# The first eight head pairs of a fused attention and MLP kernel: scores one pair ahead of values, attended rows turned one pair later, and a reordered opening

## The chip, the cores and the metric

One core of one Trainium2 chip runs the kernel. The metric is the device time of one execution in microseconds (us), as the median of several executions. A profile is one further execution of its own, taken with the hardware profiler; its times are measured from the first instruction of the span.

## The reference

`q`, `k`, `v` have 8 batches, 8 heads, 576 positions and a head size of 64. Each position attends to positions at most 32 away, to 8 global positions, and the 8 global positions attend to all. The attended rows of all heads, 4608 x 512, then go through an MLP whose inner function is h times cos(h).

```python
scores = scale * np.matmul(q, k.transpose(0, 1, 3, 2))
mask = np.abs(pos[:, None] - pos[None, :]) <= window
mask = mask | is_global[:, None] | is_global[None, :]
scores = np.where(mask, scores, -1000000000.0)
attn = exp(scores - max) / sum
x = (attn @ v), heads side by side      # 4608 x 512
h = x @ w_in                            # 512 -> 2048
out = (h * np.cos(h)) @ w_out           # 2048 -> 512
```

## The kernel before

**Tiling.** Two heads make a pair; there are 32 pairs, four of them to a batch. The steps of a pair have one letter each, and a string spells out the order in which they are issued; every engine takes its own instructions in that order.

- `k`, `q` (`local_k` L574, `local_q` L585): for the first eight pairs, 16 transposes on TensorE each (L571), for pairs 0 to 3 also 16 small matmuls that pick the rows of global positions (L308), and copies of the result out of PSUM. In `local_q` the copies are a small one on VectorE (L591) and then the large one on ScalarE (L592).
- `s` (`scores5` L597): 10 matmuls (L607) into four PSUM banks, two exponentials for the first two banks (L610) and two for the others (L614) on ScalarE, three products with the mask on VectorE (two of L611, then L615).
- `p` (`values5` L617): 20 matmuls (L622) into the one accumulator `pv`, a small sum and two reciprocals (L636 to L638), and the division that writes the attended rows `xn` (L642), all on VectorE.
- `x` (`turn_x5` L646): five transposes of `xn` (L654), copies into `xT` and a sum for the global rows on VectorE (L655, L658, L660). After a batch's last pair GpSimd writes eight columns of `xT` (L663).
- `f` fills: 128x184 matmuls on ones (L470), which write into `pv` and are overwritten. `warm` (L311) is 128x512 matmuls on ones.
- `C` turns the loaded `v` rows into fp16 (`cast_vn`, L391 on GpSimd, for the first load L393 and L394 on VectorE and ScalarE). `H` and `g` bring the global rows into `kw` and `qb`; `H1` holds two transposes (L530) and two copies (L532). `Z` builds the mask of the later pairs.
- `L`, `W`, `O`, `c`, `K` are transfers issued by GpSimd: k and q of a half batch, a quarter of `w_in`, the whole of `w_out` (L851, 2048 KB as it lands), and v, k and q cast to fp16 in device memory (L264, L268). `B` is issued by SyncE: transposing loads of such a cast half (L280, L281) and its values.
- `1`/`m` is one step of the first MLP matmul (four 128x512 matmuls, L738), with its cosine and product (L744, L745) at once or at `t`; `2` is a quarter of a 128-row step of the second (four matmuls, L755), which needs `w_out`.

**Order.** `FRONT` (L57) has pairs 0 to 7 and four MLP steps. `MID` (L49) is MLP alone while `w_out` arrives; after it `FOURTH`, `FIFTH` and `SIXTH` each run two pairs of later batches with MLP steps between, and from there `ORDER` repeats. Only two row tiles of the MLP, 32 steps of `1`, can be done until the iteration of `SIXTH`. In `FRONT` before, pair n+1's scores stand behind pair n's values, and k and q of a pair two or so ahead directly behind a pair's scores:

```
... s4 g6 g7 k6 q6 f4 x3 c4 K4 p4 s5 C3 k7 q7 f4 x4 p5 s6 W2 W3 f4 x5 p6 s7 B4 K5 O m m x6 p7 ...
```

PSUM has three banks for scores and turned rows together (tag `s`), one more for scores (`o`), two for k and q (`h`) and two for `pv`.

Of the kernel before, what the change touches and what calls it, by code (L numbers as in the profile page):

```python
# [12 lines left out]
AF = mybir.ActivationFunctionType  # L13
# [8 lines left out]
QB = 56  # L22
# [182 lines left out]
def kernel(  # L205
# [152 lines left out]
    def vn_of(s):  # L358
        return view(vn32[s // 2][:, 4 * (s % 2)], (4 * D, NK5), (1, 4 * D))
# [381 lines left out]
    def mlp_act():  # L741
        ph, g = ph_of.pop(0)
        cos = work.tile([P, TT], FP16, tag="cos", bufs=3)
        nc.scalar.activation(cos, ph, AF.Sin, bias=pio2)  # L744
        nc.vector.tensor_tensor(g, cos, ph, ALU.mult)  # L745
# [107 lines left out]
    STEPS = {"s": scores, "p": values, "x": turn_x}  # L853
    with tc.manual_schedule():

        nc.vector.memset(ones16, 1.0)
        nc.vector.memset(pio2, pi / 2.0)
        nc.vector.memset(kn[0][0:KPAD, 0:2], 0.0)
        nc.vector.memset(qn[0][64:QP, 0:2], 0.0)
# [4 lines left out]
        load_qk(0, (0, 2))  # L864
        for t in (kn[0][0:KPAD, 2:4], qn[0][64:QP, 2:4], kn[1][0:KPAD], qn[1][64:QP]):
            nc.scalar.memzero(t.rearrange("p a b c -> p (a b c)"))
        nc.scalar.activation(x_sq[:, 0:1], pio2, AF.Exp)
        nc.gpsimd.iota(tok_i, pattern=[[1, RW]], base=0, channel_multiplier=RW)
        nc.gpsimd.memset(ident16, 1.0)
        nc.gpsimd.affine_select(ident16, ident16, [[-1, P]], ALU.is_equal, 0.0, base=0, channel_multiplier=1)  # L870
        warm(WARM)
        index_rows(0)
        build_band()
        load_qk(0, (2, 4))
        for s in range(HY):
            nc.vector.memset(vn_of(s)[0:32, 0], 0.0)
        load_vn(0)
        index_rows(1)
        gather(v, vg32, 0)
        load_qk(1)  # L880
        gather(k, kg32, 0)
        gather(q, qg32, 0)
        nc.gpsimd.iota(kid_i, pattern=[[QB, NB]], base=-(G + 32), channel_multiplier=1)
        nc.gpsimd.iota(d_i, pattern=[[-1, C]], base=0, channel_multiplier=1)
        load_vn_rows(0)
        for s in range(1, HY):
            load_vn(s)
            load_vn_rows(s)
        build_ones()
        build_mask5()  # L890
# [8 lines left out]
        local_k(0)  # L899
        local_q(0)  # L900
# [36 lines left out]
        def bring(s):  # L937
# [2 lines left out]
            load_values(2 * s)  # L940
            load_values(2 * s + 1)

        LOCAL = {"k": local_k, "q": local_q}
        OTHER = LOCAL | {"g": globals_kq, "L": load_qk, "W": load_w_in, "c": lambda s: cast_half(s, "v"), "v": load_values, "n": x_squares,
                 "C": cast_vn, "V": lambda _: hold(9), "H": early_globals, "Z": steady_buffers, "f": fill, "r": load_vn, "A": later_rows, "D": later_globals, "O": load_w_out, "K": lambda s: cast_half(s, "kq" if s == 4 else "vkq"), "B": bring, "m": lambda _: one(False), "t": lambda _: mlp_act()}
        ready[0] = 1
        for step in FRONT.split():
            if step in "+-":
# [89 lines left out]
```

## Time and profile before

| | us |
|---|---|
| median of 3 runs | 368.34 (366.97 to 368.53) |
| the profiled execution | 366.35 |
| its span, first to last instruction | 364.4 |
| TensorE busy | 336.9 (92%) |
| VectorE busy | 250.2 (69%) |
| ScalarE busy | 235.6 (65%) |
| GpSimd busy | 105.7 (29%) |

The profile's page divides the span into 40 slices of 9.1 us. A row of the timeline gives start, length, engine, line, operation, output and inputs, count, and in brackets how long the engine stood idle before it and what ended that.

### The profile page before, as it was taken

What the parts mean: (1) busy time and instruction counts of PE and PEld (TensorE: products, weight loads), DVE (VectorE), ACT (ScalarE), POOL (GpSimd) and SP (SyncE); (2) the same over time, 40 slices, a digit from 0 to 9 for tenths busy, and PEclk for the clock granted to TensorE, in tenths of its full rate; (3) what the DMA queues carried; (4) which work ended last, traced back from release to release, by engine and by line L of the source; (5) the groups of instructions that cost most, each with busy time, mean ns of one, the idle gap of its engine ahead of it and who ended that gap; (6) DMA issues with size and microseconds to landing.
All of it is one profiled execution on the core that took longest, in us unless ns stands there. A gap on an engine that the chain in (4) does not pass through costs nothing.

```text
span 364.4 us, 8183 instructions
## 1 busy us (share of the span) xinstructions
PE 336.9 (92%) x3081; PEld 173.2 (48%) x3081; DVE 250.2 (69%) x607; ACT 235.6 (65%) x397; POOL 105.7 (29%) x217
## 2 busy tenths in 40 slices
PE   6597979979877999999999999999999999999993
PEld 3486735435443444444544444454544444444441
DVE  7465778966767868887878788797968444455410
ACT  5556656886732887768686777877778756644400
POOL 8634494452507322440515070502001100000000
PEclk9556789999989999999999999999999999999998
DMA  6999599999999999999999999999910000100121
GB/s 92 177 160 193 92 131 162 183 215 143 144 197 144 194 166 149 168 129 181 130 198 129 196 123 174 136 192 146 105 50 30 31 29 29 59 29 30 40 78 65
DMA packets 175655, 45.73 MB, mean 126 GB/s; under 512 B 163897, under 2 KB 170617, under 8 KB 175417
## 3 DMA queue, kind: packets, MB, share of 16 engines
q1 hardware_dynamic: 111753, 27.57, 53.6%
q0 software_dynamic: 63856, 17.57, 49.3%
q8 instruction: 26, 0.43, 0.5%
q14 instruction: 20, 0.16, 0.2%
HBM read 45.07 MB, written 20.05 MB: 179 GB/s over the span
## 4 chain that ended last, share of the span: by engine, by line
PE 68%; DMA 8%; ACT 6%; issue 6%; DVE 5%; POOL 5%; POOLq 0%; ACTq 0%
PE po L755 31%; PE ph L738 25%; DMA w_out<-in_moe_w_out_dram 8%; PE st L675 3%; PE tx L720 2%; ACT e L678 2%; POOL q L268 2%; PE pv L695 2%; ACT e L683 1%; POOL k L268 1%; PE bank L571 1%; POOL v L264 1%; PE pn L787 1%; PE st L607 1%; DVE xn L706 1%
## 5 line engine op out<-in xcount | busy, mean ns | idle before, releaser
L738 PE MATMUL ph<-xT,w_in 128*128 128x512 f16 x576 | 142.3, 382 | 1.8 <-issue 0.8
L755 PE MATMUL po<-w_out,g 128*128 128x512 f16 x576 | 140.7, 382 | 1.8 <-DMA w_out<-in_moe_w_out_dram 1.8
L744 ACT ACTIVATE cos<-ph,pio 128x512 f16<-128x512 f32 x144 | 96.8, 686 | 61.5 <-PE ph L738 59.1
L745 DVE TENSOR_TENSOR g<-cos,ph 128x512 f16<-128x512 f16 x144 | 95.5, 684 | 47.2 <-ACT cos L744 46.5
L755 PEld LDWEIGHTS <-g 128*128 128x128 f16 x576 | 55.3, 98 | 67.6 <-DMA w_out<-in_moe_w_out_dram 2.3
L738 PEld LDWEIGHTS <-w_in 128*128 128x128 f16 x576 | 54.5, 98 | 66.2 <-issue 7.3
L928 POOL COPY gate<-xn 1x1 f16<-1x1 f16 x12 | 2.2, 181 | 134.7 <-DVE xn L706 134.7
L678 ACT ACTIVATE e<-st 128x512 f16<-128x512 f32 x48 | 26.1, 595 | 16.9 <-PE st L675 16.8
L679 DVE TENSOR_TENSOR pm<-e,mask 128x512 f16<-128x512 f16 x48 | 20.3, 425 | 20.7 <-ACT e L678 19.2
L268 POOL DMA_DIRECT2D q<-in_q_dram x12 | 27.6, 2296 | 0.0
L760 ACT COPY o<-po 128x512 f32<-128x512 f32 x18 | 10.5, 585 | 22.3 <-PE po L755 22.0
L706 DVE TENSOR_TENSOR xn<-pv,r_all 128x768 f16<-128x768 f32 x24 | 23.0, 958 | 1.1
L773 ACT ACTIVATE xn<-xn 128x1536 f16<-128x1536 f16 (+1 forms) x16 | 22.8, 1423 | 0.0
L268 POOL DMA_DIRECT2D k<-in_k_dram x12 | 21.2, 1765 | 0.2 <-issue 0.2
L762 DVE COPY o<-po 128x512 f32<-128x512 f32 x18 | 12.4, 689 | 10.5 <-PE po L755 9.9
L728 POOL COPY xT<-xg 128x4 f16 x48 | 15.8, 329 | 5.5 <-DVE xT L723 2.9
L583 DVE COPY kw<-kT 128x1320 f16<-128x1320 f16 x24 | 17.1, 713 | 0.0
L610 ACT ACTIVATE e<-st 128x488 f16<-128x488 f32 x16 | 8.4, 575 | 11.8 <-PE st L607 11.8
L675 PEld LDWEIGHTS <-kw 64*128 64x128 f16 x528 | 9.2, 95 | 13.9 <-issue 8.3
L744 ACT ACT_TABLE_LOAD x12 | 15.4, 1283 | 0.2
L675 PE MATMUL st<-qb,kw 64*128 64x64 f16 x528 | 12.1, 191 | 3.5 <-POOL xT L728 2.3
L720 PEld LDWEIGHTS <-xn 128*128 128x128 f16 x144 | 9.2, 99 | 11.0 <-DVE xn L706 9.9
(168 smaller groups left out, 367.3 us busy)
## 6 DMA issues: line engine op xcount, KB each, us to landing
out_dram<-o SPq DMA_DIRECT2D x36, 256.0 KB
vw<-v SPq DMA_DIRECT2D x35, 165.0 KB
v<-in_v_dram POOLq DMA_DIRECT2D x12, 288.0 KB
k<-in_k_dram POOLq DMA_DIRECT2D x12, 288.0 KB
q<-in_q_dram POOLq DMA_DIRECT2D x12, 288.0 KB
w_in<-in_moe_w_in_dram POOLq DMA_DIRECT2D x4, 512.0 KB
w_out<-in_moe_w_out_dram POOLq DMA_DIRECT2D x1, 2048.0 KB
vn<-in_v_dram SPq DMA_DIRECT2D x16, 120.0 KB
```

The costliest lines, as they stand in the source:

```text
L268: nc.gpsimd.dma_start(dst[s].rearrange("t (h d) -> t h d", h=4), dview(src, base, (D, S), (S * D, 4), (1, D)))
L583: nc.vector.tensor_copy(to, view(kT[pr // 2 % 2][:, pr % 2], (QB, NB), (1, W)))
L675: nc.tensor.matmul(st[j // 8 * 2 + h][:, j % 8 * C : j % 8 * C + C], kp[hp, j], qp[hp, j], start=True, stop=True)
L678: nc.scalar.activation(e[:, 0:512], st[h], AF.Exp, scale=scale)
L679: nc.vector.tensor_tensor(view(pm[:, h], (1, 512)), e[:, 0:512], view(mask, (1, 512)), ALU.mult)
L706: nc.vector.tensor_tensor(view(xn, (384, 2), (D, 6), (1, D)), view(pv, (512, 2), (65, 6), (1, D)), view(rp, (6, 2), (1, 6), (0, D)), ALU.mult)
L720: nc.tensor.transpose(tx[:, n], xn[:, n], ident16)
L738: nc.tensor.matmul(ph, w_in16[:, j, f * P : (f + 1) * P], xT[:, j, t * TT : (t + 1) * TT], start=(j == 0), stop=(j == NC - 1))
L744: nc.scalar.activation(cos, ph, AF.Sin, bias=pio2)
L745: nc.vector.tensor_tensor(g, cos, ph, ALU.mult)
L755: nc.tensor.matmul(po, g16[:, f, s * P : (s + 1) * P], w_out16[:, f], start=(f == 0), stop=(f == NF - 1))
L773: nc.scalar.activation(view(xn, (BP * P, 2), (1, n)), view(xn, (BP * P, 2), (1, n)), AF.Square, accum_out=x_sq[:, s : s + 1])
```

## The change

The opening is put in another order: the first loads of k and q go out ahead of GpSimd's index patterns, memsets that only later steps need stand behind the first pair, `warm(4)` and `warm(6)` stand beside the first pair's k and q, and `w6` behind the second's; values of the second half batch are loaded ahead of the first's global rows, and the gather of q comes later. In `FRONT` the scores of pair n+1 stand in front of the values of pair n, the turn of attended rows comes behind those values and is that of pair n-1, and behind it come k and q of pair n+2. The fills between pairs 4 and 7 are gone. All of `w_in` is requested inside `FRONT`; the casts of half 4 are held (`U7`, a one-element copy on GpSimd) until the last mask product of pair 7. `w_out` is requested at the start of `MID`, which on GpSimd's queue is behind the column writes of batch 1 and the global rows of pairs 8 and 9, and the casts of half 5 come after it. `MID` has 18 steps of the first MLP matmul in place of 22; the four that are missing are taken up by `FOURTH` (two more) and `FIFTH` (two).

```diff
-MID = "+ 1 1 1 1 Z1 1 1 1 1 A0 n0 Z2 1 1 A1 kc qc 1 1 kd qd V K6 1 1 A2 n1 1 1 B5 1 1 n2 1 1 1 1 -"
+MID = "+ O 1 1 1 1 Z1 K5 1 1 1 1 A0 n0 Z2 1 1 A1 kc qc 1 1 kd qd V K6 1 1 A2 n1 1 1 B5 n2 1 1 -"
...
-FRONT = ("s0 k1 q1 C0 Z0 L2 W0 f8 s1 p0 k2 q2 f4 x0 p1 s2 C1 k3 q3 L3 W1 H0 f4 x1 p2 s3 k4 q4 H1 g4 g5 C2 k5 q5 x2 p3 "
-         "s4 g6 g7 k6 q6 f4 x3 c4 K4 p4 s5 C3 k7 q7 f4 x4 p5 s6 W2 W3 f4 x5 p6 s7 B4 K5 O m m x6 p7 t t + m m t t x7 -")
+FRONT = ("s0 k1 q1 w6 C0 L2 Q s1 p0 k2 q2 Z0 f8 s2 p1 x0 C1 W0 k3 q3 L3 H0 f4 s3 p2 x1 H1 g4 g5 k4 q4 C2 W1 f4 s4 p3 x2 "
+         "g6 g7 k5 q5 s5 p4 x3 k6 q6 C3 W2 s6 p5 x4 k7 q7 W3 s7 p6 x5 U7 c4 K4 B4 m m x6 p7 t t + m m t t x7 -")
...
+    def hold_pm(pr):
+        nc.gpsimd.tensor_copy(gate, pm_of[pr][0:1, 2 * CN - 1 : 2 * CN])
...
+        nc.vector.memset(qn[0][64:QP, 0:2], 0.0)
         nc.vector.memset(ones16, 1.0)
         nc.vector.memset(pio2, pi / 2.0)
         nc.vector.memset(kn[0][0:KPAD, 0:2], 0.0)
...
+        load_qk(0, (0, 2))
         nc.gpsimd.iota(p_i, pattern=[[0, 1]], base=0, channel_multiplier=1)
...
+        load_qk(0, (2, 4))
+        nc.scalar.activation(x_sq[:, 0:1], pio2, AF.Exp)
         warm(WARM)
         index_rows(0)
+        nc.vector.memset(vn_of(0)[0:64, 0], 0.0)
         build_band()
+        index_rows(1)
         load_vn(0)
         gather(v, vg32, 0)
         load_qk(1)
         gather(k, kg32, 0)
+        build_ones()
+        build_mask5()
+        local_k(0)
+        warm(4)
+        local_q(0)
+        warm(6)
+        for s in range(1, HY):
+            nc.vector.memset(vn_of(s)[0:32, 0], 0.0)
+        load_vn(1, 0, 3)
         load_vn_rows(0)
+        load_vn(1, 3)
+        load_vn_rows(1)
...
+        def late_gather(_):
+            gather(q, qg32, 0)
...
```

More of the change, by code (lines that the diff above doesn't have):

```diff
@@ L858 @@
         nc.vector.memset(kn[0][0:KPAD, 0:2], 0.0)
-        nc.vector.memset(qn[0][64:QP, 0:2], 0.0)
+        for t in (qn[0][64:QP, 2:4], kn[0][0:KPAD, 2:4], qn[1][64:QP], kn[1][0:KPAD]):
+            nc.scalar.memzero(t.rearrange("p a b c -> p (a b c)"))
+        load_qk(0, (0, 2))
         nc.gpsimd.iota(p_i, pattern=[[0, 1]], base=0, channel_multiplier=1)
@@ L863 @@
         nc.gpsimd.iota(kid5_i, pattern=[[KS, NK5]], base=-(G + 24), channel_multiplier=1)
[L864 to L868, printed above, removed]
         nc.gpsimd.memset(ident16, 1.0)
         nc.gpsimd.affine_select(ident16, ident16, [[-1, P]], ALU.is_equal, 0.0, base=0, channel_multiplier=1)
+        nc.gpsimd.iota(tok_i, pattern=[[1, RW]], base=0, channel_multiplier=RW)
+        load_qk(0, (2, 4))
+        nc.scalar.activation(x_sq[:, 0:1], pio2, AF.Exp)
         warm(WARM)
         index_rows(0)
+        nc.vector.memset(vn_of(0)[0:64, 0], 0.0)
         build_band()
-        load_qk(0, (2, 4))
-        for s in range(HY):
-            nc.vector.memset(vn_of(s)[0:32, 0], 0.0)
+        index_rows(1)
         load_vn(0)
-        index_rows(1)
         gather(v, vg32, 0)
@@ L881 @@
         gather(k, kg32, 0)
-        gather(q, qg32, 0)
-        nc.gpsimd.iota(kid_i, pattern=[[QB, NB]], base=-(G + 32), channel_multiplier=1)
-        nc.gpsimd.iota(d_i, pattern=[[-1, C]], base=0, channel_multiplier=1)
+        build_ones()
[7 more added lines that the diff above has]
+        load_vn(1, 0, 3)
         load_vn_rows(0)
-        for s in range(1, HY):
+        load_vn(1, 3)
+        load_vn_rows(1)
+        for s in range(2, HY):
             load_vn(s)
             load_vn_rows(s)
-        build_ones()
-        build_mask5()
         pv = ps.tile([P, 2, 512], FP32, tag="pv", bufs=1)
@@ L941, in bring @@
             load_values(2 * s + 1)
+        def late_gather(_):
+            gather(q, qg32, 0)
+            nc.gpsimd.iota(kid_i, pattern=[[QB, NB]], base=-(G + 32), channel_multiplier=1)
+            nc.gpsimd.iota(d_i, pattern=[[-1, C]], base=0, channel_multiplier=1)
         LOCAL = {"k": local_k, "q": local_q}
         OTHER = LOCAL | {"g": globals_kq, "L": load_qk, "W": load_w_in, "c": lambda s: cast_half(s, "v"), "v": load_values, "n": x_squares,
-                 "C": cast_vn, "V": lambda _: hold(9), "H": early_globals, "Z": steady_buffers, "f": fill, "r": load_vn, "A": later_rows, "D": later_globals, "O": load_w_out, "K": lambda s: cast_half(s, "kq" if s == 4 else "vkq"), "B": bring, "m": lambda _: one(False), "t": lambda _: mlp_act()}
+                 "C": cast_vn, "w": warm, "Q": late_gather, "U": hold_pm, "V": lambda _: hold(9), "H": early_globals, "Z": steady_buffers, "f": fill, "r": load_vn, "A": later_rows, "D": later_globals, "O": load_w_out, "K": lambda s: cast_half(s, "kq" if s == 4 else "vkq"), "B": bring, "m": lambda _: one(False), "t": lambda _: mlp_act()}
         ready[0] = 1
```

2 lines of the change are left out of this document (removed).

## The prediction

> **What bounds the kernel now.** I read the page, then stretches of the timeline, then the order in which each engine gets its instructions. The page and a table of stretches (busy time and count of each engine, granted clock, DMA share, GB/s) come first.
>
> ```profile
> span 364.4 us, 8183 instructions
> ...
> PE 68%; DMA 8%; ACT 6%; issue 6%; DVE 5%; POOL 5%; POOLq 0%; ACTq 0%
> ```
>
> ```profile
> core 0: us, PE busy (x) PEld busy (x) DVE busy (x) ACT busy (x) POOL busy (x), PEclk, DMA share, GB/s
> 24.00:27.00 3.00, 3.00 (x69) 2.52 (x69) 2.13 (x8) 1.55 (x4) 1.25 (x1) 0.50 1.21 197
> 58.00:79.00 21.00, 19.68 (x93) 8.62 (x90) 19.10 (x45) 17.86 (x29) 10.42 (x20) 1.00 1.54 182
> 97.60:113.40 15.80, 11.59 (x132) 5.81 (x133) 11.53 (x24) 5.97 (x12) 5.04 (x8) 0.89 1.57 172
> 113.40:133.00 19.60, 19.43 (x195) 9.53 (x196) 14.55 (x33) 13.91 (x26) 7.58 (x18) 1.00 1.65 165
> ```
>
> From 113.4 us TensorE is busy 19.43 of 19.60 us, and both kernels have the same TensorE order from the iteration of `SIXTH`, which starts there. So nothing after 113.4 us can change by much: the change is worth what it does to the moment at which that state is reached. Before it lie the eight pairs, the MLP steps of `MID`, and the stretch from 97.6, where TensorE is busy 11.59 of 15.80 us.
>
> The next rows mark the pairs: the first exponentials of pairs 1 and 7, two of seven such rows.
>
> ```profile
> 18.42 1.05 ACT L610 ACTIVATE e<-st 128x488 f16<-128x488 f32 x2 [0.21 <-PE st L607]
> ...
> 51.36 1.04 ACT L610 ACTIVATE e<-st 128x488 f16<-128x488 f32 x2 [3.25 <-PE st L607]
> ...
> 52.13 3.55 POOL L851 DMA_DIRECT2D w_out<-in_moe_w_out_dram  x1
> ...
> 80.59 1.90 PE L755 MATMUL po<-w_out,g 128*128 128x512 f16 x8 [1.84 <-DMA w_out<-in_moe_w_out_dram]
> ```
>
> Six pairs take 51.36 - 18.42 = 32.94 us, 5.49 each. `w_out` is requested at 52.13, and the second MLP matmul starts when it lands, 80.59, that is 29.2 us after pair 7's first exponential; TensorE waits only 1.84 us there, because `MID` has kept it busy. I call these two moments E7 and Y. My sum is: where E7 goes, how far behind it Y lies, and what the four postponed MLP steps cost.
>
> **The change part by part.**
>
> *The new loop of a pair.* The orders of the engines show what moves. ScalarE's large copy of q waits for VectorE's small one; the chain rows below show it, L591 ending at 40.89 and L592 starting at 40.93. Before, k and q stood right behind a pair's scores, so that L591 came directly after the mask products. In the changed kernel VectorE's order in each round is: three mask products of pair n+1, sum, reciprocals and division of pair n, three turned copies of pair n-1, and only then the small q copy of pair n+2; the scores of n+2 are next on TensorE and need that q. So each round closes a ring. Its links, from one pair of the run before:
>
> ```profile
> 39.12 0.78 DVE L611 TENSOR_TENSOR pm<-e,qT 128x488 f16<-128x488 f16 x2
> 40.26 0.56 DVE L615 TENSOR_TENSOR pm<-e,qT 128x768 f16<-128x768 f16 x1 [0.35 <-ACT e L614]
> 40.73 0.16 DVE L591 COPY qb<-bank 128x8 f16<-128x8 f16 x1
> 41.10 0.47 DVE L655 COPY xT<-tx 128x600 f16<-128x600 f16 x1 [0.20 <-PE tx L654]
> 41.49 0.15 DVE L658 COPY xT<-tx 128x8 f16<-128x8 f16 x1
> 41.55 0.18 DVE L660 TENSOR_REDUCE xg<-tx 128x8 f16<-128x32 f16 x1
> 42.14 0.15 DVE L636 TENSOR_REDUCE dg<-pv 8x2 f32<-8x8 f32 x1 [0.40 <-PE pv L622]
> 42.22 0.20 DVE L637 RECIPROCAL r_all<-pv 128x10 f32<-128x10 f32 x1
> 42.45 0.19 DVE L638 RECIPROCAL r_all<-dg 8x8 f32<-8x8 f32 x1
> 42.68 0.82 DVE L642 TENSOR_TENSOR xn<-pv,r_all 128x640 f16<-128x640 f32 x1
> ```
>
> ```profile
> 17.74 0.91 PE L607 MATMUL st<-qb,kw 64*128 64x136 f16 x10
> ...
> 38.41 1.04 ACT L610 ACTIVATE e<-st 128x488 f16<-128x488 f32 x2 [1.74 <-PE st L607]
> ...
> 40.93 0.66 ACT L592 COPY qb<-bank 128x600 f16<-128x600 f16 x1 [0.15 <-DVE qb L591]
> ```
>
> First exponential to the end of the mask products: 40.82 - 38.41 = 2.41. Sum to division: 42.14 to 43.50, 1.36. Turned copies: 41.10 to 41.73, 0.63. Small and large q copy: 40.73 to 41.59, 0.86. From the first scores matmul to the first exponential: 17.74 to 18.42, 0.68 at half clock. The sum is 5.94 us. Shown lengths of neighbours overlap by about 0.1, so I take 5.8 a round. Bounds: 5.5, if a full clock halves the 0.68, and 6.2, if nothing overlaps and each of the five handovers costs 0.05. The matmuls of values, turns, k and q lie beside VectorE's part of the ring and cost nothing; that cover holds while TensorE's work for a pair fits in a round, and at half clock with fills it filled 3.00 of 3.00 us (24 to 27), so the cover is thin. Six rounds: 34.8 us, against 32.94 before.
>
> *What the rounds have besides.* With `H1` two copies stand ahead of the small q copy on VectorE, and k and q of pair 4 need the two banks that these free.
>
> ```profile
> L532 DVE COPY kgT<-t x1: 225/225/225, 34.0 to 34.0; 128x128 f16<-128x128 f16 x1
> ```
>
> The two alone are 0.45 us; behind them now also come pair 4's transposes and ScalarE's copy of its k (0.66, as that of q above), and I take +1.4 (bounds 0.45 and 2). The cast `C3` comes behind GpSimd's eight column writes of batch 0, by my count just in pair 6's mask products:
>
> ```profile
> L391 POOL CAST vw<-vn x3: 1248/1259/2606, 24.0 to 46.7; 128x1280 f16<-128x1280 f32 x3
> ```
>
> ```profile
> 47.21 2.36 DVE L611 TENSOR_TENSOR pm<-e,qT 128x488 f16<-128x488 f16 x2
> ```
>
> The three casts took 1.25, 1.26 and 2.61 us; beside the slow one two mask products took 2.36 in place of 0.78. I take +1.4 (0 if they miss each other, 1.6).
>
> *The clock.* In 24 to 27 TensorE was busy throughout and its clock stayed at 0.50, so `warm` and `w6` hold the full clock at best through pair 0, and I count the half-clock link. The Trainium skill, "TensorE: Matmul & The Clock Gate", Part 1, says that one busy window of about 3.4 us gives full clock; this row shows more than 2 us of such busy time without it, and the same page's Part 4 says that transposes do not count as busy. By the first rule the added warming would halve the 0.68 us link, 0.34 a round and 2.0 us in all.
>
> *The opening.* Pair 1's exponentials now stand behind the cast of the first values on ScalarE. That cast came when the gathered rows landed:
>
> ```profile
> 17.18 0.56 DVE L393 CAST vw<-vn 128x768 f16<-128x768 f32 x1 [0.19 <-DMA vn<-vg]
> ```
>
> The gather is issued about as early as before; k and q of pair 0 go out ahead of the index patterns, but three tiles of the next values are queued in front of those rows on SyncE's queue. I take the landing at 16.9, and pair 1's first exponential at 17.6, 0.8 sooner than 18.42 (bounds 2.5 sooner, 0.6 later). Memsets and loads that move lie ahead of this and cost nothing while that landing ends last.
>
> So E7 = 17.6 + 34.8 + 1.4 + 1.4 = 55.2, 3.8 later.
>
> *From E7 to Y.* The request of `w_out` now waits on GpSimd for pair 7's turned rows, eight column writes and four small copies; before, these stood behind it. The last of them:
>
> ```profile
> 63.13 0.26 POOL L562 COPY qb<-qgT 128x88 f16<-128x88 f16 x1
> ```
>
> These copies ended at 63.39, which is 12.0 after E7. In the changed kernel pair 6's turn comes later too, ahead of pair 7's division on VectorE: I take 13.2. The new wait `U7` ends 2.41 after E7, with pair 7's mask; queued behind it on GpSimd are half 4's casts and these copies, whose input comes later still, so only SyncE's loads of half 4 feel it. Then `w_out` itself. While it streamed (68 to 80), GpSimd's queue moved:
>
> ```profile
> q0 software_dynamic: 2533, 2.38, 116.3%
> ```
>
> 2.38 MB in 12 us; the 2.10 MB of `w_out` take 10.6 us. With 1 us to start, 1.6 for the transposing loads of half 4 that run beside it and 0.6 for the landing, less 0.5 that issue and transfer overlap, Y = E7 + 26.5; since VectorE may also wait in `MID` for those loads (held until pair 7's mask, `U7`), I take 27.5 (25 to 30) against 29.2. `MID`'s own matmuls ended shortly before Y:
>
> ```profile
> 73.42 5.34 PE L738 MATMUL ph<-xT,w_in 128*128 128x512 f16 x24 [0.28 <-DVE g L745]
> ```
>
> 24 take 5.34 us, 0.22 each, and they end at 78.76, 27.4 after E7. Sixteen fewer (3.5 us) and pair 7 turned 1.2 later give 25.1, so `w_out` still ends last. Half 5's casts, which stood in front of `w_out`, follow it: that is the 1.7 us won here.
>
> So Y = 55.2 + 27.5 = 82.7, 2.1 later.
>
> *The postponed steps and half 5.* Four steps are 16 matmuls, 3.5 us of TensorE. Two of them fall in `FIFTH`, where TensorE waited anyway:
>
> ```profile
> 105.49 0.51 PE L720 MATMUL tx<-ident,xn 128*128 128x128 f16 x6 [1.91 <-DVE xn L706]
> ```
>
> I count 1.7 (0 to 3.5). Half 5 is 0.88 MB behind `w_out`: at the rate above 4.4 us, in small packets some 6 after Y (an estimate), and its transposing loads as long again. Pair 10's copy of k stood here:
>
> ```profile
> 96.18 0.93 DVE L583 COPY kw<-kT 128x1320 f16<-128x1320 f16 x1
> ```
>
> That is 15.6 after Y, against 12, so 3 to 4 us are spare, and I add 0.4 (0 to 4).
>
> *Sum.* 2.1 + 1.7 + 0.4 = +4.2 us on the profiled execution's 366.35 (span 364.4 and 1.95 around it): 370.6. The median of the runs shown, 368.34, lies 2.0 above that execution, so I predict a median of 372.5, 1.1% above before. About 0.5%, 1.8 us, is what a measurement of this kernel can tell from no change.
>
> **The rivals.**
>
> *Faster: the rounds are as short as VectorE's own work.* The three groups and the small copy on VectorE sum to 1.34 + 1.36 + 0.63 + 0.16 = 3.5 us. If scores ahead of values let VectorE work almost without gaps, a round is 3.8: E7 = 17.6 + 22.8 + 2.8 = 43.2, Y = 70.7, and 366.35 - 9.9 + 2.1 = 358.6 (median 360.5). It decides at a round of 5.1, below which my sum is under zero. For it: that is what such an order usually gives. Against it: the small q copy stands last in VectorE's round and ScalarE waits for it. Chance 0.13.
>
> *Given back: no change.* The rounds cost what I say, but `w_out` ahead of half 5 and the two steps in idle time win it back: Y - E7 = 25, so Y = 80.2, 0.4 sooner, and 0.5 for the steps give +0.1, 366.5 (median 368.5). For it: before, 28.5 us passed from the request of `w_out` to its landing, and its own bytes are 10.6 of them. Against: the request itself now waits behind GpSimd's copies. Chance 0.19.
>
> *Slower still: half 5 is late.* Its casts and loads land behind pair 10's turn, and each us late stands in `FOURTH` with TensorE waiting: 4 to 6 us on my sum, a median of 377 to 379. Chance 0.13.
>
> **How the numbers follow.** My forecast has 0.55, with its own range 369 to 376. The range 363 to 379 takes in the two neighbours and leaves out most of the fast rival. Faster by over 0.5%: 0.13 and a little of "given back", 0.16. Within 0.5%: most of that rival and a tenth of mine, 0.17. Slower: 0.67.
>
> **What would show it.** Right: pairs 1 to 7's first exponentials (L614 there) some 5.8 us apart; each large q copy (L596) starting right behind L595, and L595 behind the turned copies; E7 near 55; `w_out` requested near 68 and the first L759 near 83; TensorE less idle between 97 and 113. Wrong: rounds under 5 us, or L595 ready before the division; `w_out` landing more than 30 us after E7; a wait of TensorE for k of pair 10.

## The result, and the profile after

The changed kernel takes 382.38 us, the median of four runs (379.99 to 383.42), against 367.65 for the kernel before on the same chip: 1.039 times as long (95% interval 1.0333 to 1.0447). A ratio, here and below, leaves out executions in which the chip was disturbed, so it can differ a little from the quotient of the medians. The prediction was 372.5 (363 to 379): the sign was right, the size was not. The profiled execution took 379.99 us, with a span of 378.3, 13.9 more than before.

The page of the changed kernel: its span, the clock and the DMA share in 40 slices, the chain of waits by engine and by line, and one of the costliest groups.

```profile
span 378.3 us, 8195 instructions
...
PEclk9956566996999989999999999999999999999999
DMA  6999419999999999999999999999940000010021
...
PE 67%; DMA 11%; issue 7%; ACT 5%; DVE 4%; POOL 3%; SPq 1%; POOLq 0%; ACTq 0%
...
L699 PE MATMUL pv<-vw,pm 128*64 128x65 f16 x528 | 14.1, 197 | 5.2 <-DMA vw<-vg 4.6
```

The DMA row falls to 4 and 1 in the fifth and sixth slice, 38 to 57 us. And TensorE waited 4.6 us in all for values of later pairs (L699), a group that does not stand among the waits of before.

ScalarE's rows mark the opening and the rounds: the first values cast, and the first exponentials of pairs 1, 2 and 7.

```profile
21.12 0.62 ACT L398 CAST vw<-vn 128x512 f16<-128x512 f32 x1 [6.07 <-DMA vn<-vg]
21.65 1.04 ACT L614 ACTIVATE e<-st 128x488 f16<-128x488 f32 x2
...
27.37 1.05 ACT L614 ACTIVATE e<-st 128x488 f16<-128x488 f32 x2 [1.00 <-PE st L611]
...
58.03 1.05 ACT L614 ACTIVATE e<-st 128x488 f16<-128x488 f32 x2 [0.80 <-PE st L611]
```

Pair 1 comes at 21.65 (18.42 before), because ScalarE stood 6.07 us waiting for the gathered rows. Pair 7 comes at 58.03 (51.36 before): 3.23 us of its lateness come from the opening and 3.44 from the rounds.

GpSimd's rows show a second thing that is late. The changed kernel:

```profile
50.46 2.05 POOL L667 COPY xT<-xg 128x4 f16 x8 [9.64 <-DVE xg L664]
52.59 1.32 POOL L395 CAST vw<-vn 128x1280 f16<-128x1280 f32 x1
53.85 1.50 POOL L851 DMA_DIRECT2D w_in<-in_moe_w_in_dram  x2
60.50 0.18 POOL L387 COPY gate<-pm 1x1 f16<-1x1 f16 x1 [5.15 <-DVE pm L619]
60.62 0.55 POOL L264 DMA_DIRECT2D v<-in_v_dram  x1
...
71.67 1.18 POOL L855 DMA_DIRECT2D w_out<-in_moe_w_out_dram  x1
72.83 0.53 POOL L264 DMA_DIRECT2D v<-in_v_dram  x1
...
88.31 0.56 POOL L264 DMA_DIRECT2D v<-in_v_dram  x1 [6.11 <-DMA w_out<-in_moe_w_out_dram]
```

And before:

```profile
41.80 2.10 POOL L663 COPY xT<-xg 128x4 f16 x8 [4.58 <-DVE xg L660]
43.95 0.56 POOL L264 DMA_DIRECT2D v<-in_v_dram  x1
...
73.06 0.57 POOL L264 DMA_DIRECT2D v<-in_v_dram  x1
```

The rows `v<-in_v_dram` are the casts of halves 4, 5 and 6 in the changed kernel (half n holds pairs 2n and 2n+1), of halves 4 and 6 in the rows of before. Half 4 is asked for 16.7 us later (60.62 against 43.95), half 6 15.3 later. The first follows row by row: pair 3's column writes end 8.6 us later, 2.0 because pair 4 is itself later (40.39 against 38.41), the rest because the turn is now one pair later and GpSimd waits for it; a cast of 1.32, the last loads of `w_in` with 1.50, and the wait `U7` with 5.15 come in between. In that time no data moves. The table of stretches of the changed kernel (busy time and count by engine, granted clock, DMA share, GB/s):

```profile
core 0: us, PE busy (x) PEld busy (x) DVE busy (x) ACT busy (x) POOL busy (x), PEclk, DMA share, GB/s
45.00:48.00 3.00, 2.47 (x32) 1.96 (x33) 0.83 (x2) 2.19 (x5) 0.00 (x0) 0.50 0.02 3
48.00:51.00 3.00, 1.51 (x37) 1.19 (x35) 2.38 (x9) 1.15 (x2) 0.41 (x3) 0.81 0.00 0
51.00:54.00 3.00, 2.69 (x51) 2.15 (x53) 1.56 (x2) 1.98 (x5) 2.62 (x8) 0.75 0.02 5
```

The same stretch before:

```profile
48.00:51.00 3.00, 1.46 (x24) 1.00 (x24) 2.59 (x6) 0.11 (x1) 3.00 (x5) 1.00 2.25 144
```

What follows from it stands in TensorE's rows of the changed kernel: the second MLP matmul, and the values of pairs 11 and 13.

```profile
88.07 2.31 PE L759 MATMUL po<-w_out,g 128*128 128x512 f16 x5 [4.46 <-DMA w_out<-in_moe_w_out_dram]
...
118.62 0.75 PE L699 MATMUL pv<-vw,pm 128*64 128x65 f16 x22 [2.10 <-DMA vw<-vg]
...
133.72 0.72 PE L699 MATMUL pv<-vw,pm 128*64 128x65 f16 x22 [1.85 <-DMA vw<-vg]
134.36 3.56 PE L742 MATMUL ph<-xT,w_in 128*128 128x512 f16 x8
...
138.99 1.89 PE L742 MATMUL ph<-xT,w_in 128*128 128x512 f16 x8
```

Y is at 88.07, 7.5 later than before; pair 10's, 11's and 13's values are waited for, and behind the last wait eight matmuls take 3.56 us instead of 1.89. So of the span's 13.9 us, 6.7 have arisen by E7, 0.8 between E7 and Y, and 6.4 after Y.

### The profile page after: what moved, and what is told of

It reads as the page before. It is cut to its first block, busy times and chain, and to the rows that moved or that the text cites. A ratio compares the mean times of both kernels' runs of the same rounds, so it can differ in the third digit from the quotient of the medians.

```text
span 378.3 us, 8195 instructions
## 1 busy us (share of the span) xinstructions
PE 341.6 (90%) x3085; PEld 172.9 (46%) x3085; DVE 248.8 (66%) x607; ACT 238.9 (63%) x399; POOL 105.2 (28%) x218
## 4 chain that ended last, share of the span: by engine, by line
PE 67%; DMA 11%; issue 7%; ACT 5%; DVE 4%; POOL 3%; SPq 1%; POOLq 0%; ACTq 0%
PE po L759 32%; PE ph L742 26%; DMA w_out<-in_moe_w_out_dram 4%; DMA vw<-vg 3%; PE st L679 2%; PE tx L724 2%; PE pv L699 2%; DMA vn<-vg 2%; DMA vg<-in_v_dram,gidx_rows 2%; ACT e L682 1%; ACT e L687 1%; PE pn L791 1%; ACT e L614 1%; PE st L611 1%; DVE xn L646 1%
## 5 line engine op out<-in xcount | busy, mean ns | idle before, releaser
L742 PE MATMUL ph<-xT,w_in 128*128 128x512 f16 x576 | 144.4, 385 | 1.8 <-DVE g L749 1.0
L268 POOL DMA_DIRECT2D q<-in_q_dram x12 | 25.5, 2122 | 2.5 <-DMA k<-in_k_dram 2.5
L268 POOL DMA_DIRECT2D k<-in_k_dram x12 | 19.9, 1658 | 1.0 <-DMA v<-in_v_dram 0.8
L699 PE MATMUL pv<-vw,pm 128*64 128x65 f16 x528 | 14.1, 197 | 5.2 <-DMA vw<-vg 4.6
L626 PE MATMUL pv<-vw,pm 128*128 128x65 f16 (+3 forms) x160 | 11.4, 233 | 6.1 <-DVE vw L397 6.1
L732 POOL COPY xT<-xg 128x4 f16 x48 | 15.3, 319 | 5.6 <-DVE xT L727 2.9
L748 ACT ACT_TABLE_LOAD x13 | 16.7, 1283 | 0.2
L615 DVE TENSOR_TENSOR pm<-e,qT 128x488 f16<-128x488 f16 x16 | 7.4, 465 | 12.1 <-ACT e L614 11.7
```

The costliest lines, as they stand in the source:

```text
L268: nc.gpsimd.dma_start(dst[s].rearrange("t (h d) -> t h d", h=4), dview(src, base, (D, S), (S * D, 4), (1, D)))
L699: nc.tensor.matmul(pv[r0 : r0 + C, j // 6, c0 : c0 + 65], pm[:, h, j], vp[:, j, h], start=True, stop=True)
L732: nc.gpsimd.tensor_copy(xT[:, :, bass.ds(pool_idx[g] + b * S, 1)], xg[:, :, g : g + 1])
L742: nc.tensor.matmul(ph, w_in16[:, j, f * P : (f + 1) * P], xT[:, j, t * TT : (t + 1) * TT], start=(j == 0), stop=(j == NC - 1))
```

## The experiments

My theory after these rows: three things cost time. The opening's data land late; the ring through the small q copy lengthens the rounds; and GpSimd's queue, held up by pair 3's turn, starts a chain of transfers late (half 4, `w_out`, half 5, half 6) on which the second MLP matmul and the later values wait. The rivals: that pair 7's lateness alone sets everything behind it; that the half clock of TensorE, not the ring, makes the rounds; that `w_out`'s own 2 MB set Y wherever the rest stands.

All runs in one table. Ratios are to the kernel before on the same chip, with a 95% interval; the three right columns are from the profiled execution (first exponential of pairs 1 and 7, second MLP matmul; 18.42, 51.36 and 80.59 before). Different chips give the kernel before medians from 366.64 to 368.26 us, so runs on two chips are best compared by their ratios.

| run | us | before | ratio | pair 1 | pair 7 | Y |
|---|---|---|---|---|---|---|
| changed kernel | 382.38 | 367.65 | 1.039 (1.0333 to 1.0447) | 21.65 | 58.03 | 88.07 |
| e1_rows_first | 378.43 | 366.64 | 1.0323 (1.0226 to 1.042) | 21.35 | 57.54 | 87.91 |
| e2_opening_only | 372.67 | 366.64 | 1.0172 (1.0071 to 1.0272) | 23.91 | 56.35 | 86.74 |
| e3_requests_as_before | 384.22 | 366.64 | 1.0481 (1.0376 to 1.0586) | 23.84 | 61.37 | 98.36 |
| e4_kq_behind_scores | 380.44 | 366.64 | 1.0354 (1.0244 to 1.0463) | 23.80 | 59.10 | 89.58 |
| e5_hold_third_load | 379.87 | 368.26 | 1.0306 (1.0249 to 1.0363) | 19.93 | 58.11 | 88.94 |
| e6_fills_back | 385.80 | 368.26 | 1.0495 (1.0445 to 1.0546) | 21.24 | 62.89 | 96.58 |
| e7_kq_two_ahead | 381.86 | 368.26 | 1.0347 (1.0273 to 1.0421) | 23.48 | 57.19 | 89.94 |
| e8_half6_first | 381.08 | 368.26 | 1.0384 (1.0307 to 1.0462) | 21.25 | 57.66 | 86.55 |
| e9_half4_early | 375.74 | 366.75 | 1.0357 (1.022 to 1.0494) | 23.01 | 60.06 | 88.37 |
| e10_half4_wout_early | 371.19 | 366.75 | 1.022 (1.0121 to 1.0319) | 21.06 | 57.43 | 86.03 |
| e11_before_late_chain | 372.86 | 366.75 | 1.0245 (1.0106 to 1.0385) | 18.34 | 50.92 | 85.94 |
| e12_all_mended | 368.33 | 366.75 | 1.0123 (1.0046 to 1.02) | 22.12 | 54.33 | 84.47 |
| e13_opening_both | 377.39 | 367.51 | 1.027 (1.0219 to 1.0321) | 19.79 | 56.85 | 86.92 |
| e14_all_and_opening | 365.34 | 367.51 | 0.9943 (0.9915 to 0.9971) | 20.48 | 51.80 | 80.41 |
| e15_before_early_chain | 365.37 | 367.51 | 0.9958 (0.9924 to 0.9993) | 18.26 | 48.85 | 79.88 |
| e16_all_old_opening | 365.05 | 367.51 | 0.9927 (0.9899 to 0.9955) | 18.38 | 51.28 | 80.10 |

### The opening: e2, e1, e5, e13

e2 is the kernel before with the changed opening; its own FRONT keeps its order:

```diff
-FRONT = ("s0 k1 q1 C0 Z0 L2 W0 f8 ...
+FRONT = ("s0 k1 q1 w6 C0 L2 Q Z0 W0 f8 ...
```

> The kernel before with the changed opening alone; order of pairs, MID and the place of w_out's request as before. Theory (lateness of the first pair is carried to the end): pair 1's first exponential 2 to 3 us later than 18.42, pair 7's near 54, time 370 to 371. Rival (w_out was requested long before it was needed, so an opening that is late is hidden behind its landing): pair 1 late all the same, time 367.6 to 368.5.

The time rose by 6.0 us (372.67 against 366.64), more than the 370 to 371 of the theory, and pair 1, pair 7 and Y by 5.5, 5.0 and 6.1 us. The rival falls: nothing hides a late opening. It cost more here than the 3.2 us that I read from the changed kernel's trace, because the landing varies: with this opening and the third load unheld, the first values were cast between 20.5 and 23.4 us over the runs (the wait for the rows in the changed kernel ended at 21.1), against 17.5 to 17.6 with the old opening.

e1 puts the gathered rows ahead of the next values:

```diff
-        load_vn(1, 0, 3)
         load_vn_rows(0)
-        load_vn(1, 3)
+        load_vn(1)
```

> The changed kernel with one edit: the gathered rows of batch 0 are queued ahead of the first three tiles of the next values. Theory (the opening's queue order costs 3.2 us, and the end moves with it): first values cast at about 17.5 instead of 21.1, pair 1's first exponential near 18.3 instead of 21.65, pair 7's near 54.7 instead of 58.03, the end 3 us sooner, 379 us. Rival A (the loads of values 1 or the shared queues hold the rows, not their place in SyncE's order): the cast stays at 20 to 21 and the time at 382. Rival B (the opening comes earlier but the second MLP matmul waits for w_out anyway): pair 1 near 18.3, time within 1 us of 382.

The cast came at 20.8, inside the spread above, and pair 7 at 57.54. So the place of the rows in SyncE's order does not by itself make them late, as rival A has it. The time, 378.43 us, is near the theory's 379 all the same. Its ratio overlaps that of the changed kernel, and with pair 7 and Y only 0.5 and 0.2 us sooner, what its profiled execution won lies behind Y.

e5 holds the third load of k and q instead (`L2`) until the rows have landed:

```diff
+    def hold_rows():
+        nc.gpsimd.tensor_copy(gate, vn_of(0)[0:1, 0, 2 * D : 2 * D + 1])
...
-... C0 L2 Q s1 ...
+... C0 Y L2 Q s1 ...
```

> The changed kernel with one wait added: GpSimd asks for the third load of k and q (L2) only when the gathered rows of batch 0 have landed. Theory (in the changed opening that load is asked for at 13.6 instead of 17.8 and its 1.18 MB run in front of the small rows and tiles on the shared DMA engines): first values cast at 17 to 18.5 instead of 21 to 23, pair 1's first exponential at 18 to 19, pair 7's 3 to 4 us sooner, time 2 to 5 us under the changed kernel's. Rival (SyncE's own queue, three tiles of the next values ahead of the rows, holds them): the cast stays at 21 or later.

The cast came at 19.4, earlier than in every run without the hold, though not at 17 to 18.5. But pair 2 came at 27.44, as late as in the changed kernel: ScalarE stood idle for 3.26 us ahead of pair 2's k and TensorE for 0.31 to 0.46 us three times in its q, all without a releaser that the profile names. Pair 7 won nothing. e13 has both edits, and the gathers of q in front (`C0 Q Y L2`):

> The changed kernel with the gathered rows ahead of the next values, and the third load of k and q held until these rows have landed, the gathers of q in front of it as before. Theory (both orders together make the opening late): first values cast at 17 to 18, pair 1's first exponential at 17.6 to 18.5, pair 7's at 54 to 56; time 1 to 3 us less than with one of them. Rival (the DMA engines are full from 8 to 20 us whatever the order): cast at 19 or later.

GpSimd's and ScalarE's rows of e13:

```profile
18.73 0.18 POOL L391 CAST gate<-vn 1x1 f16<-1x1 f32 x1 [2.92 <-DMA vn<-vg]
19.34 0.80 POOL L275 DMA_DIRECT2D kn<-in_k_dram  x1 [0.43 <-PE t L315]
```

```profile
18.74 0.62 ACT L402 CAST vw<-vn 128x512 f16<-128x512 f32 x1 [0.98 <-DMA vn<-vg]
```

The cast is at 18.7, the third load is asked for at 19.34. Pair 1, at 19.79, and pair 7, at 56.85, just miss what was expected; the time, 377.39 us, is 1.027 of before (1.0219 to 1.0321), lower than the changed kernel's. In the changed kernel and before, the third load is the row

```profile
13.59 0.78 POOL L275 DMA_DIRECT2D kn<-in_k_dram  x1 [1.01 <-PE bank L308]
```

and

```profile
17.77 0.79 POOL L275 DMA_DIRECT2D kn<-in_k_dram  x1 [2.29 <-issue]
```

So in the changed opening the third load runs 4.2 us earlier and beside the rows that pair 0 waits for; held, it gives back 1.7 us of the cast (e5), 2.4 with the rows in front (e13) and 3.3 in e14 against e12, and in e13 1.2 us of pair 7. The Trainium skill ("DMA: Bandwidth & Descriptors", section "Queues, rings and completion order") says that each DMA engine takes turns between the queues it has work for, packet by packet; these runs agree with it, 18.3 to 18.7 with the load held and the rows first against 20.5 to 23.4. Of the 1.2 us by which e13's cast still stands behind the old opening's 17.5, SyncE's later request for the rows is 0.8 (13.82 against 12.98 before); the rest stays open.

### The rounds: e4, e7, e6

e4 puts k and q of pair n+2 directly behind the scores of pair n+1:

```diff
-... s1 p0 k2 q2 Z0 f8 s2 p1 x0 C1 W0 k3 q3 ... s5 p4 x3 k6 q6 ...
+... s1 k2 q2 p0 Z0 f8 s2 k3 q3 p1 x0 C1 W0 ... s5 k6 q6 p4 x3 ...
```

> The changed kernel with k and q of pair n+2 put right behind the scores of pair n+1, ahead of the values of pair n, so that the small copy of q no longer follows VectorE's division and turned copies. Theory (the ring through the small copy of q sets 5.7 us a round): the ring is cut to 2.4 + 0.9 + 0.7, rounds of 4.2 to 5.0, pair 7's first exponential at 50 to 54 instead of 58.03, time 375 to 378. Rival (TensorE at half clock, or VectorE's own work, sets the round): rounds stay at 5.5 to 5.8 and the time at 381 to 383.

The last three rounds were 4.14, 5.04 and 5.04 us, as the ring theory has them, at a granted clock of 0.50; but the first three were 6.41, 6.52 and 8.15, longer than the changed kernel's 5.72, 5.70 and 7.32. Six rounds together won 1.1 us, so pair 7 (59.10) and the time (380.44) missed the theory's 50 to 54 and 375 to 378. e7 leaves the first rounds and takes k and q of pairs 5 to 7 one pair earlier:

```diff
-... k4 q4 C2 W1 f4 s4 p3 x2 g6 g7 k5 q5 s5 p4 x3 k6 q6 C3 W2 s6 p5 x4 k7 q7 W3 s7 ...
+... k4 q4 k5 q5 C2 W1 f4 s4 p3 x2 g6 g7 k6 q6 s5 p4 x3 k7 q7 C3 W2 s6 p5 x4 W3 s7 ...
```

> The changed kernel with k and q of pairs 5 to 7 taken one pair earlier, so that from pair 5 on the scores of a pair no longer wait for a small copy of q of the same round. Ring: the rounds that end with pairs 5, 6 and 7 drop from 5.8, 5.6 and 6.3 to 4.2 to 5.0 even at half clock, the round of pair 4 grows by the 1.5 us of copies put into it; pair 7's first exponential 1.5 to 3.5 us sooner after pair 1's than in the changed kernel (36.4). Clock rival: rounds stay at 5.5 or more while the granted clock is 0.5.

The first exponentials of pairs 4 to 7 in e7:

```profile
44.82 1.04 ACT L614 ACTIVATE e<-st 128x488 f16<-128x488 f32 x2 [0.45 <-PE st L611]
49.70 1.05 ACT L614 ACTIVATE e<-st 128x488 f16<-128x488 f32 x2
54.59 1.05 ACT L614 ACTIVATE e<-st 128x488 f16<-128x488 f32 x2
57.19 1.05 ACT L614 ACTIVATE e<-st 128x488 f16<-128x488 f32 x2 [0.77 <-PE st L611]
```

Rounds of 4.88, 4.89 and 2.60 us came in place of 5.79, 5.59 and 6.26; the round of pair 7 has no k and q of its own left. The clock is not the reason. It was higher in e7's rounds than in the changed kernel's, but e16, further down, has the same order of these steps at half clock, and its three rounds are as long (e7, then e16):

```profile
44.82:57.19 12.37, 9.02 (x169) 6.65 (x166) 7.99 (x27) 7.78 (x17) 2.69 (x9) 0.78 0.25 41
38.92:51.28 12.36, 11.52 (x169) 8.39 (x166) 7.98 (x27) 7.88 (x16) 8.21 (x14) 0.50 1.43 182
```

With e4 this shows the ring. In the changed kernel it can be read directly: VectorE's turned copies end at 50.40, the small q copy follows them, and ScalarE's large copy that.

```profile
50.32 0.15 DVE L595 COPY qb<-bank 128x8 f16<-128x8 f16 x1
50.51 0.66 ACT L596 COPY qb<-bank 128x600 f16<-128x600 f16 x1 [0.58 <-DVE qb L595]
```

From pair 1 to pair 7 e7 won 2.7 us. The time did not follow (381.86 us; ratios 1.0347 and 1.039 with overlapping intervals): half 4 and `w_out` were asked for at 60.12 and 72.21, as in the changed kernel (60.62 and 71.67), since pair 3's turn and so GpSimd's queue had not become earlier (column writes at 54.0), and Y came at 89.94.

e6 is the clock rival: ten groups of four fills beside the steps of pairs 4 to 7.

```diff
-... f4 s4 p3 x2 g6 g7 k5 q5 s5 p4 x3 ... s6 p5 x4 ... s7 p6 x5 U7 ...
+... f4 s4 f4 p3 f4 x2 g6 g7 k5 q5 s5 f4 p4 f4 x3 ... f4 s6 f4 p5 f4 x4 ... f4 s7 f4 p6 f4 x5 U7 ...
```

> The changed kernel with ten groups of four filling matmuls put back into the rounds of pairs 4 to 7, beside scores, values and turns (they write zeros' neighbours that nobody reads). Rival to the ring (the clock: TensorE was too little busy in these rounds and stayed at half clock, which made them long): granted clock 0.8 to 1.0 from 42 to 58 us, rounds of 4.0 to 5.0, pair 7's first exponential at 53 to 55 relative to a first exponential of pair 1 at 21.65, time 3 to 5 us less. Ring: rounds stay at 5.5 to 5.9 whatever the clock (only the 0.68 us link shrinks), time within 1.5 us of the changed kernel's.

The stretch from 40 to 58 us of e6:

```profile
40.00:58.00 18.00, 12.90 (x182) 10.71 (x179) 9.29 (x29) 7.96 (x16) 4.74 (x14) 0.59 0.21 32
```

and of the changed kernel:

```profile
40.00:58.00 18.00, 11.94 (x211) 9.46 (x205) 10.44 (x33) 9.39 (x18) 5.21 (x16) 0.59 0.37 53
```

The granted clock is 0.59 in both, and the rounds became 6.95, 7.98 and 7.98 us. So the fills did not raise the clock, and they made the rounds longer, against both expectations. The rival is settled not by this run but by e7 and e16 above: the same rounds at 0.78 and at 0.50.

### GpSimd's queue: e3, e8, e9, e10, e11, e15

e3 asks for half 5 and `w_out` where the kernel before does, and has its MID:

```diff
-... U7 c4 K4 B4 m m x6 ...
+... U7 c4 K4 B4 K5 O m m x6 ...
```

> The changed kernel with the half-5 casts and w_out requested at the end of FRONT and the MID of before (22 MLP steps, B5 in its old place). Theory (the third cost is that w_out stands ahead of half 5 and half 6 then waits on GpSimd for w_out's landing): the half-6 casts are issued near 82 instead of 88, the values of pairs 10, 11 and 13 are no longer waited for, TensorE idles 3 to 5 us less after the second MLP matmul, time 376 to 379. Rival (the stalls after w_out only repeat the lateness of pair 7, whatever the order of the requests): pair 7's first exponential at 58 as in the changed kernel, and the time within 1.5 us of 382.

The half-6 cast came at 90.8, 29.4 us after pair 7 (30.3 in the changed kernel), and Y 37.0 us after pair 7 instead of 30.0; between 115 and 140 us no values were waited for. With the 3.3 us that pair 7 came later (2.2 of it the opening again) the time was 384.22, not the theory's 376 to 379. So the waits behind Y do go when half 5 is in front, but Y pays 7 us. Some 3.5 us of MLP steps, which this run's MID has again, stand in that stretch too, so e3 does not part the order of the requests from the steps; it shows no gain while the chain starts late.

e8 takes the gathers A0 and A1 behind the casts of half 6:

```diff
-... A0 n0 Z2 1 1 A1 kc qc 1 1 kd qd V K6 1 1 A2 ...
+... n0 Z2 1 1 kc qc 1 1 kd qd V K6 A0 A1 1 1 A2 ...
```

> The changed kernel with the four gathers of later rows (A0, A1) put behind the casts of half 6 in MID instead of in front. Theory (the first cast of half 6 stands eight requests behind w_out on GpSimd's queue and waits until w_out has landed, which makes the values of pairs 10 to 13 late): that cast is issued near 82 instead of 88.3, without the 6.1 us wait, and the waits for values between 112 and 134 us (4.55 us of TensorE) shrink to under 2; time 2 to 4 us less. Rival (the data of half 6 stand behind w_out's on the same DMA queue whenever they are asked for): the issue moves to 82 and the waits and the time stay, within 1.5 us.

GpSimd's rows of e8:

```profile
81.01 0.51 POOL L264 DMA_DIRECT2D v<-in_v_dram  x1
...
86.76 1.00 POOL L331 DMA_INDIRECT kg<-in_k_dram,gidx_rows  x1 [0.65 <-DMA w_out<-in_moe_w_out_dram]
```

The issue moved to 81 as the theory had it, and the rival's outcome came all the same: values were still waited for 0.82, 0.31 and 2.73 us (0.60, 2.10 and 1.85 in the changed kernel), and the time is the changed kernel's within the interval. The wait of 6.11 us was real but not the cause.

e9 puts the last loads of `w_in` and half 4 ahead of pair 3's turn, without `U7`; e10 puts `w_out` there as well:

```diff
-... k5 q5 s5 p4 x3 k6 q6 C3 W2 s6 p5 x4 k7 q7 W3 s7 p6 x5 U7 c4 K4 B4 ...
+... k5 q5 W2 W3 c4 K4 s5 p4 x3 k6 q6 C3 s6 p5 x4 k7 q7 s7 p6 x5 B4 ...
```

```diff
-MID = "+ O 1 1 1 1 Z1 K5 ...
+MID = "+ 1 1 1 1 Z1 K5 ...
...
-... W2 W3 c4 K4 s5 ...
+... W2 W3 c4 K4 O s5 ...
```

> The changed kernel with the last two loads of w_in and the casts of half 4 put ahead of pair 3's turn on GpSimd, and without the wait for pair 7's mask. Theory (GpSimd's order, not the rounds, sets the second MLP matmul: those loads stood behind pair 3's column writes, 50.5 instead of 41.8, and the DMA engines were idle from 45 to 54): half 4's casts are issued near 42 to 47 instead of 60.6, DMA moves data from 42 on, half 4's loads are done before w_out is asked for near 71, w_out lands 11 to 13 us after its request instead of 16.4, second MLP matmul 3 to 5 us sooner relative to pair 7, time 3 to 5 us less than the changed kernel's. Rival (w_out is bound by its own 2.1 MB and the place of its request): it lands 16 us after its request as before, time within 1.5 us.

> As the run with half 4 early, and w_out requested there too, right behind half 4's casts. Theory (the DMA chain): w_out lands before 75, the second MLP matmul starts as soon as MID's matmuls end, about 25.6 us after pair 7's first exponential (30.0 in the changed kernel), the values of pairs 10 to 13 are not waited for, time 6 to 10 us less than the changed kernel's, 372 to 376. Rival (the rounds set the time; E7 at 58 is what is late): second MLP matmul 4 us sooner, but the end at most 3 us sooner.

In e9 `w_out` landed 15.5 us after its request, where the theory said 11 to 13 and the rival 16; yet no values were waited for up to 150 us. Its time, 375.74, is lower than the changed kernel's, but the ratios overlap. In e10 the time was 371.19 us, with pair 7 at the same place (57.43): about 6 us under the changed kernel by the ratios (1.022, 1.0121 to 1.0319), 11 by the medians. GpSimd's rows of e10:

```profile
41.65 0.55 POOL L264 DMA_DIRECT2D v<-in_v_dram  x1
...
44.37 2.25 POOL L855 DMA_DIRECT2D w_out<-in_moe_w_out_dram  x1
49.87 2.04 POOL L667 COPY xT<-xg 128x4 f16 x8 [3.25 <-DVE qb L595]
```

The column writes stand at 49.87, as late as ever, but the transfers are in front of them. Y moved only to 28.6 us after pair 7, not 25.6: TensorE no longer waited for `w_out`, but for VectorE in `MID` (2.84 us). The span is 10.5 us shorter than the changed kernel's, 2.0 of it by Y and 8.5 behind it. The rival (pair 7 sets the time) falls.

The stretch from Y to the end of the span says the same of all runs whose MID is that of the changed kernel but for the requests: it is 285.0 to 290.6 us where half 4 is asked for only behind pair 7's mask (the changed kernel, e1, e4 to e8, e13), and 281.8 to 284.4 where that is done ahead of pair 3's turn (e9, e10, e12, e14, e16). What a late chain costs there varies: e1 has the 285.0, and waited 1.1 us for values in place of 4.6, with half 4 as late (60.13).

e11 makes the opposite edit in the kernel before: the chain is held until pair 6's mask is done.

```diff
-... f4 x3 c4 K4 p4 s5 C3 k7 q7 f4 x4 p5 s6 W2 W3 f4 x5 ...
+... f4 x3 p4 s5 C3 k7 q7 f4 x4 p5 s6 U6 c4 K4 W2 W3 f4 x5 ...
```

> The kernel before, with the casts of half 4, the last two loads of w_in and so all that follows on GpSimd held until pair 6's mask is done (about 5 us later), and nothing else moved. Theory (the DMA chain from half 4's casts to w_out sets the second MLP matmul): pair 7's first exponential stays within 1 us of 51.4, half 4's casts near 49 instead of 43.95, second MLP matmul 4 to 5 us later (85), time 3 to 5 us more than before. Rival (pair 7's exponential sets it): second MLP matmul at 80 to 81.5, time within 1 us of before.

Rows of e11 on GpSimd and TensorE:

```profile
49.16 0.56 POOL L264 DMA_DIRECT2D v<-in_v_dram  x1
```

```profile
85.94 3.21 PE L759 MATMUL po<-w_out,g 128*128 128x512 f16 x8 [6.82 <-DMA w_out<-in_moe_w_out_dram]
```

Pair 7 stays at 50.92, half 4 comes 5.2 us later, Y 5.35 later, and the time rises by 6.1 us (by the medians; ratio 1.0245, 1.0106 to 1.0385). This is the cleanest of the runs: GpSimd stands with 5% in the chain of waits of the page before, and yet a wait put on it costs its whole length.

e15 moves the same transfers forward in the kernel before:

```diff
-... s4 g6 g7 k6 q6 f4 x3 c4 K4 p4 ... s6 W2 W3 f4 x5 ...
+... s4 g6 g7 W2 W3 c4 K4 k6 q6 f4 x3 p4 ... s6 f4 x5 ...
```

> The kernel before with the last two loads of w_in and the casts of half 4 put ahead of pair 3's turn on GpSimd; nothing else moved. Theory (the chain of DMAs bounds before too, TensorE waited 1.84 us for w_out): half 4's casts issued near 38 to 40 instead of 43.95, w_out no longer waited for, second MLP matmul 1.5 to 3 us sooner, time 364 to 366.5. Rival (TensorE's matmuls of MID end at 78.8 and bound it): at most 1.8 us sooner, or nothing if the transfers slow the products of the rounds.

Half 4 is asked for at 38.16, and Y comes without a wait at 79.88, 0.7 us sooner, where the theory said 1.5 to 3. The time is 0.9958 of before (0.9924 to 0.9993). So before, the chain was only just the bound: taking its wait of 1.84 us away leaves TensorE's own matmuls of `MID`, as the rival had it.

### Sums: e12, e14, e16

e12 has the edits of e1, e7 and e10 together; e14 the hold of e13 besides; e16 is e12 with the opening of the kernel before.

> The changed kernel with three edits at once: gathered rows ahead of the next values, k and q of pairs 5 to 7 one pair earlier, and the last w_in loads, half 4 and w_out ahead of pair 3's turn. Theory (three separate costs that add): pair 7's first exponential at 54 to 56, second MLP matmul at 79 to 82, no wait for values after it, time 367 to 371. Rival (one of them hides the others): no better than the run with half 4 and w_out early.

> The run with all three edits, and the hold of the third load besides. Theory: pair 1 3 to 4 us earlier than in that run (22.12), the second MLP matmul 2 to 3 us earlier, time 365 to 367, at or just under the kernel before. Rival (half 4's transposing loads hold MID, which waited 2.85 us for VectorE): second MLP matmul as there, 84, time 367.5 to 369.

> The run with all three edits, but with the opening of the kernel before. Theory (the changed opening costs 3 to 5 us that nothing gives back): first values cast at 17.2 to 17.6, pair 7's first exponential at 50 to 52, second MLP matmul at 80 to 82, time 363 to 366. Rival (the opening is hidden behind half 4 and w_out in this order): pair 7 at 50 to 52 all the same, second MLP matmul at 83 or later, time 367 to 369.

e12 took 368.33 us, about 10 less than the changed kernel by the ratios; its Y is at 84.47, not at 79 to 82. The times of e14 and e16 are as the theory has them, 365.34 and 365.05 us, 0.6% and 0.7% under the kernel before, though e14's pair 1 came 1.6 us earlier than e12's, not 3 to 4. They are faster than both kernels, and they are alike: once the transfers are in order, the old opening is worth no more than the changed one with its third load held. But e15, with the old order of pairs and only its transfers moved, is at 0.9958, and the intervals overlap: that the new order of pairs wins anything by itself is not shown. TensorE's rows of e16 show what bounds Y next:

```profile
70.13 10.13 PE L742 MATMUL ph<-xT,w_in 128*128 128x512 f16 x40 [2.85 <-DVE g L749]
80.10 1.89 PE L759 MATMUL po<-w_out,g 128*128 128x512 f16 x8
```

No wait for `w_out` is left; ahead of the last forty matmuls of `MID` TensorE waits 2.85 us for VectorE.

## Why the prediction was wrong

Of the span's growth by 13.9 us, 4.2 were forecast. Of the 9.7 that are missing, 2.8 lie ahead of E7, 2.5 between E7 and Y, and 4.3 behind Y.

- **The loop of a pair: right.** 5.8 us a round was forecast; the rounds without extra work took 5.72, 5.70, 5.79 and 5.59. `H1` cost 1.5 (forecast 1.4), `C3` 0.5 (forecast 1.4, bounds 0 and 1.6). Six rounds took 36.4 us, forecast 37.6. e4, e7 and e16 show that the small q copy closes the ring.
- **The opening: wrong.** "I take the landing at 16.9, and pair 1's first exponential at 17.6" (at most 0.6 later than before): it was 21.65. I had counted the three tiles in front of the rows on SyncE's queue, which alone (e1) change nothing that stands out of the spread, and not the third load of k and q, which the new order lets GpSimd ask for 4.2 us earlier. That is 4.05 us on the sum, of which the rounds gave 1.2 back: E7 at 58.03 against 55.2.
- **From E7 to Y: wrong by 2.5 us.** The request of `w_out` came 13.6 us after E7 (forecast 13.2) and the end of `MID`'s matmuls 25.6 after it (25.1). But I let the landing follow the request by 14.3 us, and it took 16.4. The 1 us to start, 1.6 for half 4's loads and 0.6 for the landing in that sum rested on no row; with half 4's loads out of the way (e9) it still took 15.5, and what fills the rest stays open.
- **The transfers as a chain: the step that failed most.** I measured everything from E7, as if the transfers hung on it, and wrote of the wait `U7` that "only SyncE's loads of half 4 feel it", and of half 5 that "3 to 4 us are spare, and I add 0.4 (0 to 4)". In fact half 4, `w_out`, half 5 and half 6 move one behind the other, and the engines idled from 45 to 54 us because GpSimd stood at pair 3's turn, one pair later by the change itself. 9.64 us of that wait are in the trace; in the prediction I named GpSimd's column writes of batch 1 in front of `w_out`, but for those of batch 0 only the cast `C3` behind them, and not `W2`, `W3` and `K4`. It shows behind Y: 6.4 us instead of the 2.1 that I had for half 5 and the postponed steps. e10 and e11 show the cause, from both sides. The rival "half 5 is late" named this stretch, and its 4 to 6 us fit the 4.3 that are missing there; but pair 10 waited only 0.60 us, and pairs 11 and 13 waited 2.10 and 1.85.
- **The clock.** That TensorE would at best keep the full clock through pair 0 was right: it stood idle from 16 to 20 us, the clock was 0.50 soon after, and it stayed there while TensorE was busy 5.88 of the 6 us from 22 to 28.
- **The postponed steps.** No run tries their 1.7 us alone. With the chain early they do not show: behind Y, e9, e10, e12, e14 and e16 take 281.8 to 284.4 us with these steps, the kernel before 283.8 without them.

## What to carry to other kernels

When a step is moved later on one engine, list every transfer that is issued behind the instruction that waits for it, on the queue of the issuing engine, and follow the whole chain of bytes, not only the transfer that lands last today. Look at the DMA row of the page for stretches where nothing moves: an idle transfer engine early in a kernel that later waits for data is the lost time, though the waits that show it stand 40 to 80 us further on. And an early load that is not yet needed costs the small one beside it that is.

## What the runs showed of the hardware

- On GpSimd's queue in these runs a request waits for the landing of the eighth request before it, whatever it carries. Whether the chip or the program's way of waiting sets the eight, no run shows. Three rows show the wait: in the changed kernel the cast of half 6 stands eighth behind `w_out` and waited 6.11 us; with the gathers moved (e8) the second gather stands eighth and waited until `w_out` had landed; before, it was the first gather of v, in the row below. The next three requests of the changed kernel fit: each stands eighth behind a cast of half 5, and its wait (0.84, 2.52 and 0.89 us) ended with a cast of the same tensor.

```profile
80.82 1.02 POOL L331 DMA_INDIRECT vg<-in_v_dram,gidx_rows  x1 [3.86 <-DMA w_out<-in_moe_w_out_dram]
```

- The clock was halved behind a wait of 1.85 us, and not behind a longer one of 2.10. The changed kernel's stretches around pair 11's wait, and from pair 13's on:

```profile
116.00:120.00 4.00, 1.90 (x33) 1.22 (x33) 1.71 (x7) 0.04 (x1) 0.00 (x0) 1.00 1.05 216
132.00:134.00 2.00, 0.28 (x8) 0.22 (x10) 1.28 (x4) 0.04 (x1) 0.00 (x0) 1.00 1.51 277
134.00:136.00 2.00, 2.00 (x24) 0.89 (x24) 1.46 (x4) 0.00 (x0) 0.00 (x0) 0.61 1.04 199
136.00:138.00 2.00, 2.00 (x6) 0.76 (x5) 0.70 (x2) 0.73 (x2) 1.86 (x4) 0.54 1.26 205
```

The Trainium skill ("TensorE: Matmul & The Clock Gate", Part 1) speaks of one idle window of about 3.4 us; here a stretch that was busy 0.28 of 2.00 us came before the half clock, which then lasted some 3 us. The measurement decides: a shorter wait can cost too, here some 1.7 us on eight matmuls, and the length of the wait alone does not tell which one does.
